# Fourteen rounds of an attention kernel issued in other orders, and six subtractions moved from GpSimd to VectorE

## The chip, the cores and the metric

The kernel runs on one core of a Trainium2 chip. Its time is the device time of one execution in microseconds, as the median of three runs. A profile is one further execution, with its own time. The core's engines each work through an instruction queue of their own, in order: TensorE (PE; its weight loads are listed as PEld), VectorE (DVE), ScalarE (ACT), GpSimd (POOL) and SyncE (SP), which here only issues transfers. An instruction waits at the head of its queue until what it needs from other engines is there, and everything behind it in that queue waits with it.

## What is computed

A gate mixes attention and a gated feed-forward block over the same input: 2048 positions, width 448, 16 heads of 28, 1792 hidden units, all float32.

```python
q, k, v = split_heads(x @ wqkv)                      # 16 heads of 28
p = softmax(einsum("bhqd,bhkd->bhqk", q, k) * 28 ** -0.5)
a = merge_heads(einsum("bhqk,bhkd->bhqd", p, v)) @ wo
gate = x @ W_gate
b = ((gate * (gate > 0)) * (x @ W_up)) @ W_down
g = sigmoid((x * gate_w).sum(-1, keepdims=True))
return g * a + (1 - g) * b
```

## The kernel before

Every operand of the projections is split into a high and a low part, and products are summed in PSUM from several terms, 11 for a projection. The program has three stages: the projections of the input (with the first maxima of scores mixed in), 32 rounds of attention, and a tail with the second half of the feed-forward block and the output.

A round `v` works on half of the 16 key blocks of head `v // 2`, for all four groups of 512 queries. One string per round (`ROUNDS`) sets the order of work, one letter a step, and it is written out by hand for rounds 0 to 10 and 29 to 31; rounds 11 to 28 take `R11` and `R12` in turn. The loop over the letters issues each step's instructions to their engines' queues in that order; no scheduler moves them afterwards. The letters are:

- `s` (`score`): two 128x512 matmuls into a pair of PSUM banks, and one read of it on ScalarE. Most scores are read by the exponential, with a bound that sits in the operands already. Those of a raw query group (`RAW`: group 3 in round 0, groups 3 and 2 in all others) are copied with their sign turned.
- `b` (`block_min`): VectorE takes the minimum of raw scores, straight from the PSUM pair for all but the first of four.
- `A` (`all_max`): seven VectorE instructions make of it one bound for every query; the last, a transpose, spreads it over the partitions (`rm`).
- `g` (`take_max`): subtracts that bound from a quad, four blocks of raw scores, 128x2048, in SBUF. GpSimd does it.
- `e`, `E` (`take_exp`): the exponential of half a quad, or of a whole one, on ScalarE.
- `P`, `Q` (`pv`): 16 products each with V, four of them side by side in the array. The profile has two records for each, 64 a round.
- `m` (`smax`): two matmuls and a VectorE maximum that prepare the bound of a later head; `n` (`smax_end`) finishes it.
- `x`: one matmul of the projections (rounds 0 to 3) or of the feed-forward block's gate and up products. After 11 of them a bank is full. ScalarE takes the gate product (`rl`), and VectorE multiplies the up product by it (`h`).
- `w`, `N`, `c`, `f`, `D`: splitting of weights, normalisation, the rescaling of a head's two halves, and the first weights of the tail.

The scores and the maxima share three pairs of PSUM banks in turn (`ps_w`), so each user of a pair waits for the readers of the user three before it. The `x` products share two single banks (`ps_x`) with the products with V. Scores run four steps ahead of their round, so a round opens with the four raw scores of its query group 2, and ends with the four of group 3 of the next round. At an odd round's start ScalarE copies the finished product with V (`ox<-po`); at an even one's VectorE adds it.

Of the kernel before, what the change touches and what calls it, by code (L numbers as in the profile page):

```python
# [8 lines left out]
F32 = mybir.dt.float32  # L9
# [3 lines left out]
OP = mybir.AluOpType  # L13
AX = mybir.AxisListType
# [4 lines left out]
P = 128  # L19
# [7 lines left out]
NF = F // P  # L27
NB = 4
# [24 lines left out]
R0 = "bsxxsbxxxxbsxxssAxxxxxxsxxsxxxmsxxgsxxxxmxsxxsxbgxxxxxxxxbEsxxemxbxxxmxeAPQ"

R1 = "nsgmsxxssNxxxxxbgxxEbbsmxxxxxxssxsxxxxAsxmxsxxxsExxxmxgmsxxxmxxxxxExmsxmgxxxxxscbssbebAPefQ"

R2 = "smsxbxxssxbxxxsgxxxsbxgxxxsmsxAxsxsxsxsmxxxxxsxmxEgxxxmmsxxbxxxsexsexgexxxxxbmexxebAxmePQ"

R3 = "nsgmsxxsgswxxbxwxxbbeAxxssxxxxxsxsxxsexmxxwxmxsNxxxsxmExmxxmxsgxxxxsxxxgmemsxxxxexsxbcbxsPebAfeQw"
# [3 lines left out]
R5 = "gsxsxxsbgsxbxxxxxwwxxxbxsmxxwxwsxssAxxxxsmxsxxxnssmxgxExmxmsxxNxxEmxxxmssgEbePbcmsbfeAxxxxxQ"

R6 = "wssbsxxxxgbsxbxxgxxxxxwxssxxxmwxsmxxsAxsxxxsxxsmxexsxeemxxxgxmsgxxemxxxmxeesseePsbwxbmQbxAx"

R7 = "ssxNxbwxgssxxxbbxxxxxAxwxswxsxxxsxxxssxmxxxxwEgxmmxnxsxsxxmsxEmxxgxmsxemxxxmgsxbsexbsecbfeAPQ"

R8 = "wxsmsbxgxxsxxswxxgxbxsbexxxsxxxssxxxAxgssxxxmxxsxmsxxxmexsxxmemegxwsxbEPmsxxbxemxsexbxAwxQ"

R9 = "sxwsNxxggswsxxxxxxxxxbsxbbxsxxsxsAxxsxxsxgemmxgxsxsxxxmxemxsxmxnEwxxwxxxmsmbEPemscxxsebfbxxAQ"

R10 = "wsxxxgssxxgxsbxxxxbxwxxxsbxwxsxxsxxsxsAsgxsxxxxmxxxemsxmxexxxmsxExxmxsmbgxxsPEebemmsbAwQ"

R29 = "sxxsxsxxxbxgxsxxbsxExsxxxxxxxxxbxssxsxAxxxsxgNxxsxsxxxssxxxxgxsxxxExxxbxgxxbxExsexxcxexfxPbAQn"

R30 = "sgsxxsbxxsxxxxxbxxgxEbxxxxxsxxxxxsssxxxxxsxxsxAsxxxxexgxxxxsxsExxxsexxxbgxxxxsexbxxsexDDbxPQA"

R31 = "sxsxxsxxxbxxxxxsbbxxxxxxxgsxxxxsxxssxxxxAsxxsxxgxgxgExxxDxxxxNxxxExxEsexcexxsxxfxxxDxPQ"
# [20 lines left out]
def gated_mix_kernel(ctx, tc, x, wq, wo, wgu, wd, out):  # L100
    nc = tc.nc
# [141 lines left out]
    AT, QUAD, slots = {}, {}, iter(range(10 ** 6))  # L243
# [43 lines left out]
    def move(dst, src):  # L287

        nc.vector.tensor_reduce(dst, src.unsqueeze(len(src.shape)), axis=AX.X, op=OP.min)

    def all_max():
        v, j, quads = todo_all.pop(0)
        to = ((0, 11) if j == 2 else (9, 10))[v % 2]
        a, b = (1 - v % 2, 9) if j == 2 else (1, 9 + v % 2)
        nc.vector.tensor_reduce(MN[:, 1:3], R2.pop((v, j)).rearrange("p a (b r) -> p a b r", r=32), axis=AX.X, op=OP.min,  # L295
                                apply_transpose=True)
        move(MN[:64, 3:5], MN[64:, 1:3])
        move(MN[:32, 5:9], MN[32:64, 1:5])
# [4 lines left out]
        nc.vector.transpose(RM[v, j], MN[:, to].unsqueeze(2).to_broadcast([P, 16, 32]))  # L303
        todo_sub.extend((v, j, q) for q in quads)

    def take_max():
        v, j, q = todo_sub.pop(0)
        m = RM[v, j].unsqueeze(1).to_broadcast([P, 4, TB])
        nc.gpsimd.tensor_tensor(QUAD[q], QUAD[q], m, op=OP.subtract)  # L309
# [55 lines left out]
    with tc.tile_pool(name="qkv", bufs=1) as pa:  # L365
# [170 lines left out]
        m, first, ahead = 0, 6, MAXIMA  # L536
# [59 lines left out]
    done = (starts[-1] - QP) // (2 * NT)  # L596
# [67 lines left out]
    RS = {}  # L664

    def rescale(v, part):

        h = v // 2
        if v % 2 == 0:
            return  # L670
        rows = slice(64, P)
        if part == 0:
            RS[h] = fe.tile([P, TB], F32, name=f"rs_{h}", tag="rb", bufs=1)
            for r, a, b in ((slice(64, 96), 11, 0), (slice(96, P), 10, 9)):
                nc.gpsimd.tensor_tensor(MN[r, 1], MN[r, a], MN[r, b], op=OP.subtract)
            nc.vector.transpose(RS[h][rows], MN[rows, 1].unsqueeze(2).to_broadcast([64, 16, 32]))
# [98 lines left out]
    for v, order in enumerate(ROUNDS):  # L775
        small_things(2 * v)
        if v == 2 * H - 3:
            early_d()
        ns = 0
        for o in order:  # L780
            if o == "s":
                ns += 1
                if ns == 6:
                    small_things(2 * v + 1)
                if ns in (1, 9) and v % 2 == 0:
                    loads(v // 2, load_k if ns == 1 else load_q)
# [153 lines left out]
    def down(i):  # L940
# [6 lines left out]
        if f == NF - 1:  # L947
# [75 lines left out]
```

## Time and profile before

| what | value |
|---|---|
| median of three runs | 1185.54 us (1185.16 to 1185.97) |
| the profiled execution | 1184.21 us, of which 1182.4 us from the first to the last instruction |
| granted TensorE clock | 0.999 of full speed |
| ScalarE, exponentials of raw scores (L320), all of them | 257.7 us |
| GpSimd, subtractions of the bound (L309) | 126 of 4.635 us |
| rounds 1 to 31 | 121.1 to 985.8 us of the span |
| the tail | 985.8 to 1182.4 us |

In the lines of the profile, an instruction is named by its line in the code, its engine and what it writes and reads: `s` scores, `sm` maxima, `qk` and `gu` the `x` products, `po` the products with V, `r` the running minimum, `rm` the spread bound, `P` and `V` the quads (two of the ten quad slots lie in a part of `V`). A row of the timeline gives start, length, engine, line, operation, and then, in brackets, how long the engine had been idle and what ended that. A row of the windows gives a stretch, its length, and each engine's busy time with the number of its instructions. A row of groups ends with busy time, mean length in ns, and idle time ahead of the group.

### The profile page before, as it was taken

What the parts mean: (1) busy time and instruction counts of PE and PEld (TensorE: products, weight loads), DVE (VectorE), ACT (ScalarE), POOL (GpSimd) and SP (SyncE); (2) the same over time, 40 slices, a digit from 0 to 9 for tenths busy, and PEclk for the clock granted to TensorE, in tenths of its full rate; (3) what the DMA queues carried; (4) which work ended last, traced back from release to release, by engine and by line L of the source; (5) the groups of instructions that cost most, each with busy time, mean ns of one, the idle gap of its engine ahead of it and who ended that gap; (6) DMA issues with size and microseconds to landing.
All of it is one profiled execution on the core that took longest, in us unless ns stands there. A gap on an engine that the chain in (4) does not pass through costs nothing.

```text
span 1182.4 us, 17006 instructions
## 1 busy us (share of the span) xinstructions
PE 1175.0 (99%) x6183; PEld 821.2 (69%) x6183; DVE 894.1 (76%) x1173; ACT 877.2 (74%) x1054; POOL 743.3 (63%) x325
## 2 busy tenths in 40 slices
PE   9999999999999999999999999999999999999998
PEld 6886666666666666666666666666666667899997
DVE  6577898888988898989898888889898553444242
ACT  5237889899999988888888887888888885322121
POOL 5323667888988886777777766767676784422020
PEclk9999999999999999999999999999999999999999
DMA  9994565636373754343446535153444437644342
GB/s 322 280 394 142 186 210 172 185 124 196 117 216 108 205 167 139 119 128 92 119 136 212 140 102 153 49 152 109 139 154 156 129 100 231 209 152 118 115 134 75
DMA packets 70667, 188.85 MB, mean 160 GB/s; under 512 B 13958, under 2 KB 20558, under 8 KB 65678
## 3 DMA queue, kind: packets, MB, share of 16 engines
q1 hardware_dynamic: 65624, 167.31, 45.9%
q0 software_dynamic: 4480, 19.99, 4.5%
q8 instruction: 48, 0.79, 0.3%
q10 hardware_dynamic: 480, 0.47, 0.1%
q14 instruction: 35, 0.29, 0.1%
HBM read 126.96 MB, written 60.96 MB: 159 GB/s over the span
## 4 chain that ended last, share of the span: by engine, by line
PE 96%; DVE 1%; DMA 1%; ACT 1%; issue 0%; SPq 0%; DVEq 0%; ACTq 0%
PE gu L633 24%; PE s L330 20%; PE po L692 19%; PE acc L927 12%; PE sm L224 10%; PE v L469 3%; PE wo L886 3%; PE qk L641 3%; PE qk L454 2%; DVE r L280 1%; DMA wr<-wq 0%; DMA X<-x_d 0%; ACT P L336 0%; ACT V L336 0%; SPq L414 0%
## 5 line engine op out<-in xcount | busy, mean ns | idle before, releaser
L309 POOL TENSOR_TENSOR P<-P,rm 128x2048 f32<-128x2048 f32 x102 | 470.8, 4635 | 107.9 <-DVE rm L303 84.1
L633 PE MATMUL gu<-X,wg 128*128 128x512 f32 x1232 | 358.9, 395 | 0.1
L228 DVE TENSOR_REDUCE mx<-sm 128x1 f32<-128x1024 f32 x256 | 302.9, 1217 | 43.0 <-PE sm L224 42.1
L330 PE MATMUL s<-Q,K 128*128 128x512 f32 x1024 | 315.9, 403 | 1.7 <-DVE mx L228 0.9
L633 PEld LDWEIGHTS gu<-X,wg 128*128 128x128 f32 x1232 | 231.2, 188 | 57.6 <-issue 1.7
L330 PEld LDWEIGHTS s<-Q,K 128*128 128x128 f32 x1024 | 180.7, 188 | 82.4 <-DVE r L280 10.4
L336 ACT ACTIVATE P<-s 128x1024 f32<-128x1024 f32 x204 | 202.2, 1028 | 42.0 <-PE s L330 39.6
L692 PE MATMUL po<-P,V 128*32 128x512 f32 x1640 | 227.4, 594 | 0.0
L334 ACT ACTIVATE P<-s 128x1024 f32<-128x1024 f32 x206 | 201.4, 1040 | 14.1 <-PE s L330 13.1
L320 ACT ACTIVATE P<-P 128x1024 f32<-128x1024 f32 (+1 forms) x182 | 208.5, 1171 | 0.5 <-POOL P L309 0.2
L224 PE MATMUL sm<-K,Q 128*128 128x512 f32 x520 | 163.2, 400 | 0.1
L280 DVE SCALAR_TENSOR_TENSOR r<-s,r 128x1024 f32<-128x1024 f32 x124 | 151.6, 1223 | 13.6 <-ACT P L336 6.0
L692 PEld LDWEIGHTS po<-P,V 128*32 128x32 f32 x1640 | 62.6, 110 | 113.3 <-issue 109.6
L692 PE MATMUL po<-V 128*32 128x512 f32 x408 | 136.2, 594 | 0.0
L309 POOL TENSOR_TENSOR V<-V,rm 128x2048 f32<-128x2048 f32 x24 | 111.2, 4635 | 26.1 <-DVE rm L303 22.6
L224 PEld LDWEIGHTS sm<-K,Q 128*128 128x128 f32 x520 | 91.9, 188 | 34.1 <-ACT P L334 4.6
L136 ACT ACTIVATE hh<-hr 128x512 fp32r<-128x512 f32 x52 | 32.8, 632 | 109.5 <-PE acc L927 109.4
L142 DVE TENSOR_TENSOR hh<-hr,hh 128x512 fp32r<-128x512 f32 x52 | 47.3, 915 | 72.6 <-ACT hh L136 72.5
L927 PE MATMUL acc<-WD,hh 128*128 128x448 f32 x480 | 99.5, 366 | 0.0
L927 PEld LDWEIGHTS acc<-WD,hh 128*128 128x128 f32 x480 | 90.2, 188 | 7.3 <-DVE hh L142 0.2
L280 DVE SCALAR_TENSOR_TENSOR r<-s,P 128x1024 f32<-128x1024 f32 x50 | 61.1, 1223 | 33.3 <-ACT P L336 33.0
L295 DVE TRANSPOSE_TENSOR_REDUCE mn<-r 128x32 f32<-128x1024 f32 x63 | 78.1, 1239 | 1.3
(93 smaller groups left out, 1135.5 us busy)
## 6 DMA issues: line engine op xcount, KB each, us to landing
wg<-ws_d SPq DMA_DIRECT2D x42, 896.0 KB
K<-qk_d SPq DMA_DIRECT2D x32, 448.0 KB
X<-x_d SPq DMA_DIRECT2D x56, 256.0 KB
h_d<-h SPq DMA_DIRECT2D x56, 256.0 KB
Q<-qk_d SPq DMA_DIRECT2D x62, 224.0 KB
hr<-h_d SPq DMA_DIRECT2D x52, 256.0 KB
ws_d<-wg SPq DMA_DIRECT2D x14, 896.0 KB
x_d<-X POOLq DMA_DIRECT2D x8, 1024.0 KB, 15.2
```

The lines of the kernel that those rows point to most:

```text
L224: nc.tensor.matmul(ps[:, c, :], Q[h][:, u * P:(u + 1) * P], K[h % 3][:, k0:k0 + TB], start=True, stop=True)
L228: nc.vector.tensor_reduce(to, ps, axis=AX.XY, op=OP.max)
L280: nc.vector.scalar_tensor_tensor(r, ps, -1.0, before, op0=OP.mult, op1=OP.min)
L295: nc.vector.tensor_reduce(MN[:, 1:3], R2.pop((v, j)).rearrange("p a (b r) -> p a b r", r=32), axis=AX.X, op=OP.min, apply_transpose=True)
L309: nc.gpsimd.tensor_tensor(QUAD[q], QUAD[q], m, op=OP.subtract)
L320: nc.scalar.activation(q, q, AF.Exp, scale=-SCALE)
L330: nc.tensor.matmul(ps[:, c], K[h % 3][:, k * P:(k + 1) * P], Q[h][:, j * TB:(j + 1) * TB], start=True, stop=True)
L334: nc.scalar.activation(dst, ps, AF.Exp, scale=SCALE)
L336: nc.scalar.activation(dst, ps, AF.Copy, scale=-1.0)
L633: nc.tensor.matmul(ps, WS[i][:, s, a], xf(i // NF, b), start=(n == 0), stop=(n == NT - 1))
L692: nc.tensor.matmul(po[32 * j:32 * j + 32], V[:, h // 4 % 2, k, h % 4], AT.pop((v, k, j)), start=(k == k0), stop=(k == k0 + NK // 2 - 1))
L927: nc.tensor.matmul(ACC[i // NF][t][:, :D], HH[i][:, a, t * P:(t + 1) * P], wd_high_low(f, b), start=(f == 0 and n == 0), stop=(f == NF - 1 ...
```

## The change

Fourteen strings are replaced (rounds 0 to 10 and 29 to 31). Each round keeps its number of `s`, `m`, `x`, `b`, `A`; some exponentials are issued as halves in place of wholes or the reverse. A new letter `G` is a `g` whose subtraction VectorE does: once in rounds 4 and 29, twice in rounds 30 and 31, six in all. Code that allows a third raw query group is added, which no entry of `RAW` uses, and a guard at the end that changes nothing here, since 52 of the 56 hidden units are finished in the rounds as before.

```diff
-RAW = [(3,), (3, 2), (3, 2), (3, 2)]
+RAW = [(3,)] + [(3, 2)] * 31
...
-R4 = "smsxxxssbxxxxswxgbwxxbxsxxgsxsAxxsswxxmxgsxexmsxxxsxxmxexsmgxxsxbxxxxxxExxbsExembxemwPQAm"
+R4 = "smsxxxsxsbxxxxxxxgsxxbbwswxxxsxsAsxwxgmxxmxxxxExsxsxsGxsExxmgxxmxxxxmsxbxxsxsbbPEAeemmwQ"
...
     def all_max():
         v, j, quads = todo_all.pop(0)
-        to = ((0, 11) if j == 2 else (9, 10))[v % 2]
-        a, b = (1 - v % 2, 9) if j == 2 else (1, 9 + v % 2)
+        c = 12 if j == 1 else 0
+        to = ((12, 21), (0, 11), (9, 10))[j - 1][v % 2]
+        a, b = (c + 1 - v % 2, c + 9) if j < 3 else (1, 9 + v % 2)
...
-    def take_max():
+    def take_max(engine):
         v, j, q = todo_sub.pop(0)
         m = RM[v, j].unsqueeze(1).to_broadcast([P, 4, TB])
-        nc.gpsimd.tensor_tensor(QUAD[q], QUAD[q], m, op=OP.subtract)
+        engine.tensor_tensor(QUAD[q], QUAD[q], m, op=OP.subtract)
         todo_exp.append(q)
...
-            elif o == "g":
-                take_max()
+            elif o in "gG":
+                take_max(nc.gpsimd if o == "g" else nc.vector)
...
-            (split_wd, 4), (fetch_w, 8), (split_wd, 5), (fetch_w, 9), (fetch_h, 7), (gate_up, done + 1)]
+            (split_wd, 4), (fetch_w, 8), (split_wd, 5), (fetch_w, 9), (fetch_h, 7)]
+    if done + 1 < NB * NF:
+        todo.append((gate_up, done + 1))
```

Three places of the order follow, on TensorE and on VectorE. The first is TensorE at the opening of round 1, behind round 0's products: `s_8_2` to `s_14_2` are its four raw scores, `sm` a maximum, `mt` the small transpose of step `n`, `qk` the `x` products. Before:

```order
L236 MATMUL mt_1112<-ident,m_711 8x128
L330 MATMUL s_8_2_1120<-Q_107,K_104 128x512 x2
L224 MATMUL sm_1127<-K_106,Q_810 128x512 x2
L330 MATMUL s_10_2_1131<-Q_107,K_104 128x512 x2
L641 MATMUL qk_1135<-X_119,wb_113 128x512 x2
L330 MATMUL s_12_2_1139<-Q_107,K_104 128x512 x2
L330 MATMUL s_14_2_1143<-Q_107,K_104 128x512 x2
```

And now:

```order
L331 MATMUL s_8_2_1113<-Q_107,K_104 128x512 x2
L224 MATMUL sm_1119<-K_106,Q_810 128x512 x2
L236 MATMUL mt_1123<-ident,m_711 8x128
L331 MATMUL s_10_2_1130<-Q_107,K_104 128x512 x2
L331 MATMUL s_12_2_1135<-Q_107,K_104 128x512 x2
L331 MATMUL s_14_2_1143<-Q_107,K_104 128x512 x2
```

The two `qk` matmuls that stood between the second and the third score now come behind the fourth, and `mt` has moved behind the first maximum; `s_12_2` takes the banks of `s_8_2`.

The second is VectorE at the opening of round 30, behind round 29's last bound: `ox` is the sum of a head's products, `mh` the end of step `n`, `r_30_2` the minima of the round's raw scores, `h` a hidden unit's product, `rq` the reciprocal of row sums. Before:

```order
L303 STREAM_TRANSPOSE rm_3_8478<-mn 128x512
L700 TENSOR_TENSOR ox<-po_8454,ox 128x512
L142 TENSOR_TENSOR mh_8501<-mt_8499,mh_8501 8x128
L280 SCALAR_TENSOR_TENSOR r_30_2_8524<-s_2_2_8512,P_2_0_8506 128x1024
L280 SCALAR_TENSOR_TENSOR r_30_2_8524<-s_4_2_8520,r_30_2_8524 128x1024
L280 SCALAR_TENSOR_TENSOR r_30_2_8524<-s_6_2_8528,r_30_2_8524 128x1024
L652 TENSOR_TENSOR h_8564<-gu_1_8543,rl_8540 128x512
```

And now:

```order
L304 STREAM_TRANSPOSE rm_3_8476<-mn 128x512
L702 TENSOR_TENSOR ox<-po_8452,ox 128x512
L142 TENSOR_TENSOR mh_8499<-mt_8497,mh_8499 8x128
L310 TENSOR_TENSOR P_3_0_8395<-P_3_0_8395,rm_3_8476 128x2048
L280 SCALAR_TENSOR_TENSOR r_30_2_8539<-s_2_2_8510,P_2_0_8505 128x1024
L280 SCALAR_TENSOR_TENSOR r_30_2_8539<-s_4_2_8515,r_30_2_8539 128x1024
L280 SCALAR_TENSOR_TENSOR r_30_2_8539<-s_6_2_8525,r_30_2_8539 128x1024
```

A subtraction from a raw quad, `P_3_0`, has come in ahead of the three minima; the other quad of the same bound, `P_3_1`, stays on GpSimd.

The third is VectorE in round 4, from the round's first bound on: `mx` are the maxima of step `m`. Before:

```order
L303 STREAM_TRANSPOSE rm_2_2020<-mn 128x512
L228 TENSOR_REDUCE mx_1658<-sm_2040 128x1
L228 TENSOR_REDUCE mx_1658<-sm_2054 128x1
L652 TENSOR_TENSOR h_2063<-gu_1_2000,rl_1986 128x512
L228 TENSOR_REDUCE mx_1658<-sm_2077 128x1
L228 TENSOR_REDUCE mx_1658<-sm_2088 128x1
```

And now:

```order
L304 STREAM_TRANSPOSE rm_2_2022<-mn 128x512
L228 TENSOR_REDUCE mx_1654<-sm_2037 128x1
L228 TENSOR_REDUCE mx_1654<-sm_2043 128x1
L653 TENSOR_TENSOR h_2048<-gu_1_1986,rl_1979 128x512
L310 TENSOR_TENSOR P_2_0_1944<-P_2_0_1944,rm_2_2022 128x2048
L228 TENSOR_REDUCE mx_1654<-sm_2083 128x1
L228 TENSOR_REDUCE mx_1654<-sm_2092 128x1
L228 TENSOR_REDUCE mx_1654<-sm_2101 128x1
```

Here too a subtraction stands ahead of the round's later maxima; the second quad of this bound stays on GpSimd, behind two of the bound before it.

More of the change, by code (lines that the diff above doesn't have):

```diff
@@ L51 @@
 R12 = "gsmsxxxxssebxxbbxxxsxxxxmxAexxssxgsxxsxxsxxmxxsxxemsmexgxexmxxxmsxmxexsbxsgebsebAPQ"
[L53 to L59, printed above, removed]
-R4 = "smsxxxssbxxxxswxgbwxxbxsxxgsxsAxxsswxxmxgsxexmsxxxsxxmxexsmgxxsxbxxxxxxExxbsExembxemwPQAm"
@@ L63 @@
[L63 to L79, printed above, removed]
+R0 = "xsbxxsxsbbxsxxxsxAxxxxsxxxsxxgsmgxxxxxxsxmxsbxxxxxxxsxxbexmxxxexsxxxbxEAmPQ"
+R1 = "smnssbbgsxxxxbAexxsxxxsxxxxgsxxsxxxsxmxsxmxNxgsxexmxsEmgxxxmxxxmxsxxmExxcxssxxxxbsebxfbxeAPQ"
@@ new lines @@
+R2 = "smsxxxsxxbxxbsgxsxxsbAxxxxxssxsgxsxxxmxxsxxmsxxEmxxxmxsxmxxsxbxxsbxxxgxxmEsgEexbAxexmPQ"
+R3 = "NsmnsxbgxssxxxebgbxxsAwxxsxxxxwsxsswgxxxxxsxmxxsxxmesexxmxxxxxcsxmgxsxbxsbsbeAxexxfxxxxeexxPmmemQw"
+R4 = "smsxxxsxsbxxxxxxxgsxxbbwswxxxsxsAsxwxgmxxmxxxxExsxsxsGxsExxmgxxmxxxxmsxbxxsxsbbPEAeemmwQ"
+R5 = "sxNxsxsgsbxxbxxxbxwxxxxxsmxxmxEsxmxxsxwxsAxxswgxxssmxxxxxxEmsxxmnxgxsmmExxxscsbxbxsgbAPefeQw"
+R6 = "sxxxsxxxssxxbbgxwbxxxsxxxemxxxmAsgxsxxxsxsxxxsmxxxesxmsxexxgmxsmexxxgxmexssePbeexbxmswQwbAw"
@@ new lines @@
+R7 = "sswxNssxxbbxbxgxxxxwxxxsxxsxEmmxswxmxxxssxxxssAxxmxgxxxmesmxexnsmgsbxxxxExcxssgfxbxbexxewAmPQ"
+R8 = "gwxsmsxxxbsxgbxxsxxxbexsAxxgsxxxxsxxssxxsxxmxxsgxxexmxxsmeewxxxwEmmxmPesmxsxxsxbxbexxsbAwQ"
+R9 = "NwgsxsxbxsxxsbxxxxxxwsbxxgswxAgxssxsxxsxxmxsxxsxmnsxxmmmxxxcmgxxExxEswxxbxxsPbmEesmxxxbeAxfQ"
+R10 = "wssxsxbgxwxbxxxsxxxxbxsxxwxxsxxsgxAxssxxxxssxxxxmxsEgmxxmxsxxmxmgxxxExsxsbsEPebebmmmwAQ"
+R29 = "NsxxssxsGxxxxxxxbEbxgxxbxsExxxxsxxxxxxsxxxxxAsxxxsxsgxxsxxxsxsxexxxxcssxxgexxbbxsxexxxxexfPbAQn"
@@ L81 @@
+R30 = "GsssxxxxxsxexxexxxbbbxxxxxAxxxxxsxsxsxxxsxxxgsxxxgxsxsGxsxxxxsxxxsEEexsxxxesbxbDbxxxxDxxxxPQA"
+R31 = "sgxxsbxxxxxsgDxxxbxsxxxxbxsxxsAxxxxxxNsExsxexxGxxsxxsxxxxxxxxxxxGexxxxxcxexxeesexsfxxxDPQ"
 ROUNDS = [
@@ L202, in raw @@
     def raw(v):
-        return RAW[v] if v < len(RAW) else RAW[len(RAW) - 2 + v % 2]
+        return RAW[v]
     def rows_of(h):
@@ L292, in all_max @@
         v, j, quads = todo_all.pop(0)
-        to = ((0, 11) if j == 2 else (9, 10))[v % 2]
-        a, b = (1 - v % 2, 9) if j == 2 else (1, 9 + v % 2)
-        nc.vector.tensor_reduce(MN[:, 1:3], R2.pop((v, j)).rearrange("p a (b r) -> p a b r", r=32), axis=AX.X, op=OP.min,
+        c = 12 if j == 1 else 0
+        to = ((12, 21), (0, 11), (9, 10))[j - 1][v % 2]
+        a, b = (c + 1 - v % 2, c + 9) if j < 3 else (1, 9 + v % 2)
+        nc.vector.tensor_reduce(MN[:, c + 1:c + 3], R2.pop((v, j)).rearrange("p a (b r) -> p a b r", r=32), axis=AX.X, op=OP.min,
                                 apply_transpose=True)
-        move(MN[:64, 3:5], MN[64:, 1:3])
-        move(MN[:32, 5:9], MN[32:64, 1:5])
+        move(MN[:64, c + 3:c + 5], MN[64:, c + 1:c + 3])
+        move(MN[:32, c + 5:c + 9], MN[32:64, c + 1:c + 5])
         nc.vector.tensor_reduce(MN[:32, to], MN[:32, a:b].rearrange("p a b -> p b a"), axis=AX.X, op=OP.min)
@@ L588, in gated_mix_kernel @@
     att = stk.enter_context(tc.tile_pool(name="att", bufs=1))
-    MN = att.tile([P, 12, 16], F32, name="mn")
+    MN = att.tile([P, 22, 16], F32, name="mn")
     nc.vector.memset(MN[:, 0], 0.0)
@@ L670, in rescale @@
             return
-        rows = slice(64, P)
+        more = 1 in raw(v)
+        rows = slice(0 if more else 64, P)
         if part == 0:
             RS[h] = fe.tile([P, TB], F32, name=f"rs_{h}", tag="rb", bufs=1)
-            for r, a, b in ((slice(64, 96), 11, 0), (slice(96, P), 10, 9)):
+            for r, a, b in ((slice(0, 32), 21, 21), (slice(32, 64), 21, 12), (slice(64, 96), 11, 0), (slice(96, P), 10, 9))[0 if more else 2:]:
                 nc.gpsimd.tensor_tensor(MN[r, 1], MN[r, a], MN[r, b], op=OP.subtract)
-            nc.vector.transpose(RS[h][rows], MN[rows, 1].unsqueeze(2).to_broadcast([64, 16, 32]))
+            nc.vector.transpose(RS[h][rows], MN[rows, 1].unsqueeze(2).to_broadcast([P - rows.start, 16, 32]))
         else:
```

## The prediction

> **What bounds the kernel now.** I read the page first, for the engine that sets the end, then four stretches as windows and the chain of work that ended last, for how long TensorE stood, and last the timelines of three round openings.
>
> ```profile
> PE 1175.0 (99%) x6183; PEld 821.2 (69%) x6183; DVE 894.1 (76%) x1173; ACT 877.2 (74%) x1054; POOL 743.3 (63%) x325
> ...
> PE 96%; DVE 1%; DMA 1%; ACT 1%; issue 0%; SPq 0%; DVEq 0%; ACTq 0%
> ```
>
> TensorE is busy for 99% and holds 96% of the chain. The change adds and removes none of its matmuls, so it moves the time by TensorE's waits alone. These are larger than the missing 1%, because a matmul's end is modelled and covers a short wait. So I count matmuls against time. The pace, from the chain:
>
> ```profile
> 510.66 7.00 PE po L692 x64
> ...
> 972.07 3.74 PE gu L633 x16
> ```
>
> I use 7.0 us for the 64 records of a round's products with V, and 0.233 us for each 128x512 matmul (3.74 / 16 is 0.234). The windows are cut where a round's last product ends: rounds 1 to 10, round 14 alone, rounds 11 to 28, rounds 29 to 31; first the length, then each engine's busy time.
>
> ```profile
> 121.08:406.88 285.80, 285.61 (x1544) 184.81 (x1543) 248.89 (x324) 261.72 (x305) 234.07 (x100) 1.00 0.54 168
> 490.69:517.66 26.97, 26.97 (x151) 17.54 (x150) 23.78 (x31) 23.39 (x26) 19.03 (x5) 1.00 0.59 167
> 406.88:905.12 498.24, 498.10 (x2719) 317.28 (x2719) 442.01 (x586) 435.05 (x491) 359.64 (x109) 1.00 0.45 136
> 905.12:985.83 80.71, 80.68 (x449) 53.11 (x447) 41.90 (x65) 71.62 (x76) 64.31 (x23) 1.00 0.38 114
> ```
>
> Rounds 1 to 10 have 898 matmuls by their strings (418 x; two for each of 160 s and 80 m): 209.2 + 70.0 = 279.2, so **6.6 us of waits, 0.66 a round**. Round 14 has 85: 19.8 + 7.0, so 0.17, the best on show. Rounds 11 to 28, which keep their order, have 1557: 362.8 + 126.0, so 9.4, 0.52 a round. Rounds 29 to 31 have 253: 58.9 + 21.0, so 0.8. At round 14's pace 4.9 us of the first stretch and 0.3 of the last could go. Round 0 has two more places:
>
> ```profile
> 94.80 0.75 issue
> ...
> 103.30 0.93 ACT P L334
> 104.23 0.04 issue
> 104.27 0.73 PE s L330 x2
> ```
>
> The chain leaves TensorE for 0.75 us ahead of the round's first score; the score at 104.27 waits for a copy on ScalarE, for at most as long. So **the orders can win at most 4.9 + 0.3 + 1.5 = 6.7 us**.
>
> **What sets a round's opening.** It has four raw scores. Three pairs of PSUM banks go round, so the third user after a score waits for that score's readers. Round 1, on TensorE, then on VectorE:
>
> ```profile
> 120.99 0.71 PE L330 MATMUL s<-Q,K 128*128 128x512 f32 x2
> ...
> 122.93 1.05 PE L330 MATMUL s<-Q,K 128*128 128x512 f32 x3
> ```
> ```profile
> 123.77 1.23 DVE L280 SCALAR_TENSOR_TENSOR r<-s,P 128x1024 f32<-128x1024 f32 x1 [0.34 <-ACT P L336]
> 125.10 2.55 DVE L280 SCALAR_TENSOR_TENSOR r<-s,r 128x1024 f32<-128x1024 f32 x2
> ```
>
> The first score's banks came free, after ScalarE's copy, for the matmul at 122.93, 1.94 us in: the time of 8 matmuls. The other three come free as VectorE's minima end, at 125.00, some 126.35 and 127.65: 4.0 to 6.7 us in, the time of about 18, 23 and 29 matmuls. These times are set by ScalarE and VectorE. **An order that has issued fewer matmuls by then waits for the difference**, 0.233 us each. I take the same four marks for every round (even ones open behind an addition on VectorE in place of a copy on ScalarE) and count the matmuls ahead of the four users, rounds 1 to 10:
>
> - before: 8/19/21/29, 9/17/22/28, 8/19/21/28, 9/17/23/27, 11/23/25/30, 10/21/23/28, 11/23/26/31, 10/20/25/30, 9/20/24/28, 12/22/26/30. The largest shortfalls are 2, 1, 2, 2, 0, 1, 0, 0, 1, 0: in all 9.
> - after: 6/16/21/27, 9/18/22/29, 8/17/21/27, 9/21/25/30, 9/22/24/28, 12/20/25/30, 7/20/24/27, 10/21/25/31, 11/19/23/27, 13/20/26/30. They are 2, 1, 2, 0, 1, 0, 2, 0, 2, 0: in all 10.
>
> **Part by part**, against the profiled execution's 1184.21 us, 1.33 under the median of 1185.54; the sum is added to either alike.
>
> 1. Openings of rounds 1 to 10: one matmul more, +0.23 us. Rounds 4 and 6 win; 5, 7 and 9 lose. Round 29 had 14/18/22/34 and has 9/22/28/36: -0.23.
> 2. Round 0. ScalarE's order up to the copy at 103.30 is the same in both, and so is what holds it. Ahead of the matmul that waits for it the old order has 35 of the round's matmuls, the new one 33: +0.47. One is put ahead of the first score, into the wait of 0.75; that buys nothing, since the later wait ends no sooner.
> 3. Six subtractions move from GpSimd to VectorE: one each in rounds 4 and 29, two each in 30 and 31.
>
> ```profile
> L309 POOL TENSOR_TENSOR P<-P,rm 128x2048 f32<-128x2048 f32 x102 | 470.8, 4635 | 107.9 <-DVE rm L303 84.1 <-DVE rq L707 12.9 <-ACT P L320 4.9
> ...
> L142 DVE TENSOR_TENSOR hh<-hk,hh 128x512 fp32r<-128x512 f32 x4 | 2.7, 674 | 2.4 <-ACT hh L136 2.4
> ...
> L278 DVE TENSOR_TENSOR r<-P,r 128x1024 f32<-128x1024 f32 x2 | 2.5, 1226 | 0.2
> ```
>
> VectorE takes 0.674 us for 512 columns and 1.226 for 1024, so about 1.226 + 2 x 0.552 = 2.3 for 2048, against 4.6 on GpSimd. But both operands lie in SBUF, and such an instruction does not run beside one of GpSimd. In the tail:
>
> ```profile
> 1127.47 2.42 POOL L145 TENSOR_TENSOR on<-or,on 128x1024 fp32r<-128x1024 f32 x1 [32.74 <-ACT on L136]
> 1127.94 2.50 DVE L142 TENSOR_TENSOR hh<-hr,hh 128x512 fp32r<-128x512 f32 x1 [3.17 <-ACT hh L136]
> ```
>
> VectorE's subtraction took 2.50 us in place of 0.674: it ended at 1130.44, 0.55 after GpSimd's. VectorE's present work in rounds 1 to 31 has an operand in PSUM or no second one, so the rounds don't show this yet. A moved subtraction costs VectorE between 2.3 and 2.3 + 4.6 = 6.9 us, and what stands behind it comes late. Round 30, GpSimd and then VectorE:
>
> ```profile
> 932.43 9.21 POOL L309 TENSOR_TENSOR P<-P,rm 128x2048 f32<-128x2048 f32 x2 [0.76 <-DVE rm L303]
> ```
> ```profile
> 931.57 0.71 DVE L303 STREAM_TRANSPOSE rm<-mn 128x512 f32<-128x512 f32 x1
> 932.98 0.69 DVE L700 TENSOR_TENSOR ox<-po,ox 128x512 f32<-128x512 f32 x1 [0.70 <-PE po L692]
> 933.59 0.27 DVE L142 TENSOR_TENSOR mh<-mt,mh 8x128 fp32r<-8x128 f32 x1
> 935.58 1.23 DVE L280 SCALAR_TENSOR_TENSOR r<-s,P 128x1024 f32<-128x1024 f32 x1 [1.72 <-ACT P L336]
> ```
>
> GpSimd starts on the first of two subtractions as soon as `rm` is there, 932.43. The change gives the other to VectorE behind `mh`, at 933.86, and ahead of the round's minima. It would stand until 937.1 and end near 939.3 (2.2 after, as in the tail). The minima then end at 940.5, 941.8 and 943.0 and not from 936.8 on: 7.7, 9.0 and 10.2 us into the round, the time of 33, 39 and 44 matmuls, where the new order has 29, 32 and 35. Shortfall 9 matmuls, 2.1 us. An `rm` that comes earlier shortens it, to nothing if by more than 2 us; I take +1.9.
>
> Round 4 stands as follows. GpSimd has two subtractions ahead, until 221.3 where its present rows have them; VectorE comes to its own after `rm`, two maxima and a product, near 221.4.
>
> ```profile
> 212.04 13.82 POOL L309 TENSOR_TENSOR P<-P,rm 128x2048 f32<-128x2048 f32 x3
> ```
>
> Behind it stand three maxima, whose first pair of banks is wanted 17.5 us into the round. If VectorE is first, nothing waits; if GpSimd has just begun its third, the maxima come 6.9 us later and TensorE waits 3.6. I take +1.2, a meeting a third of the way, as the two come so close. Round 29's comes right behind `rm`, ahead of GpSimd; round 31's two come when GpSimd has finished: nothing, and at most 2.9 (below).
>
> The Trainium skill ("SBUF — State Buffer", section "SBUF: two separate sides") says that GpSimd and VectorE hold a pair of ports exclusively, and that the later one blocks for the whole instruction. The rows at 1127 agree; by a free sharing of the ports this term would be about nothing.
>
> 4. The other waits of rounds 1 to 10, 6.6 - 9 x 0.233 = 4.5 us, lie at restarts and among later maxima. The new order may remove 2.8 of it (4.9 less the openings' 2.1) or add as much. The nearest row is the unchanged rounds', 0.52 against 0.66; reaching it gives -1.4. I take half, -0.7.
>
> The products wait for no subtraction now, and in the new order the nearest subtraction stands 6.7 us of TensorE's time ahead of its product (6.4 before): nothing. Were that cover gone, GpSimd's 4.6 us would show at a product. The tail is the same.
>
> Sum: 0.23 - 0.23 + 0.47 + 1.9 + 1.2 - 0.7 = **+2.9 us**: 1187.1 for the profiled execution, 1188.4 for the median.
>
> **The rivals.**
> - *The two engines do not collide* (0.32): `rm` comes two us earlier, or the ports let both through. Terms 1, 2 and 4 are left, -0.2: 1185.3, no change. For it: 6.9 us is the worst meeting, and the new orders shift both engines. Against it: in round 30 GpSimd needs nothing but `rm`, and VectorE has two instructions in between.
> - *The waits do go* (0.18): faster. Copies and minima come free for the new users in all rounds as in round 14 now, and nothing collides: half of the 6.7 us goes, 1182.2. It decides where the marks 8/18/23/29 move with the order. Against it: 10 matmuls of shortfall where there were 9.
> - *A hidden unit's product stands behind a subtraction too*: its bank is wanted again after 11 matmuls of the other and some six of scores, 4.0 us, so a full 6.9 costs 2.9 more: 1191.3. It is the upper part of the forecast's own case.
> - *The change does not do what it says*: at the openings the distance is not larger. That is in the forecast already.
>
> **How the numbers follow.** A measurement of this kernel tells about 0.2%, 2.4 us, from no change. The forecast (0.50) reaches from 1186.5 to 1191.3 and lies for the most part, not all, beyond 1187.9: slower 0.40. Within: its lower part and the first rival, 0.42. Faster: 0.18. The range runs from the middle of the faster case to just under the product's: 1182.4 to 1190.8.
>
> **What would show it.** Subtractions on VectorE that take 2.3 us where GpSimd rests, and 4 to 7 where it works, the first of round 30 above all; behind it TensorE waits near 940 to 943. No waits at the opening of round 4 and some near its end. The windows: rounds 1 to 10 within 284 to 288 us, 29 to 31 over 82. Wrong would be subtractions of 2.3 us beside a busy GpSimd, or banks that are free after 6 or 16 matmuls in round 1.

## The result, and the profile after

The changed kernel takes 1194.26 us (median, 1192.97 to 1194.62) against 1185.76 us before: a ratio of the means of 1.0068, 95% interval 1.0055 to 1.0081. The forecast was 1188.4 (1182.4 to 1190.8): the sign was right, the size too small by 5.9 us, and the time lies 3.5 us above the range. The profiled execution of the changed kernel took 1192.97 us with a span of 1191.2, 8.76 us over the one before.

Engines and chain on the page of the changed kernel:

```profile
PE 1178.0 (99%) x6183; PEld 820.8 (69%) x6183; DVE 921.3 (77%) x1179; ACT 877.5 (74%) x1054; POOL 721.5 (61%) x319
...
PE 90%; DVE 3%; DMA 2%; ACT 2%; issue 1%; POOL 0%; SPq 0%; ACTq 0%; DVEq 0%; POOLq 0%
```

TensorE has the same 6183 records, and holds 90% of the chain where it held 96%. These 6% are not the size of its waits: at a wait the chain goes over to the work of the engine that ended it. Two of the moved subtractions now lie on the chain, nearly whole (start, length, engine, tile, line):

```profile
223.01 6.22 DVE P L310
...
940.31 5.63 DVE P L310
```

The waits are read from the windows, cut as before where a round's last product ends (length first): rounds 1 to 10, 11 to 28, 29 to 31.

```profile
121.71:413.53 291.82, 288.16 (x1547) 185.17 (x1544) 255.62 (x325) 261.56 (x302) 229.14 (x100) 0.99 0.52 163
413.53:911.50 497.97, 497.88 (x2722) 317.23 (x2719) 441.66 (x585) 435.12 (x491) 360.44 (x110) 1.00 0.45 137
911.50:994.60 83.10, 81.44 (x451) 52.84 (x447) 60.87 (x70) 71.97 (x79) 46.98 (x18) 1.00 0.33 111
```

Rounds 1 to 10 take 6.0 us more than before (285.80), rounds 29 to 31 2.4 more (80.71); the unchanged rounds 0.3 less (498.24), and round 0 ends 0.6 later (121.08). The sum is 8.8. By single rounds, as waits, that is a round's length between starts on TensorE less 0.231 us for each of its matmuls and 7.0 for its products (so worked out from the records, us; the prediction's 0.233 a matmul would make every sum lower, rounds 1 to 10 before at 6.6 in place of 8.1). The column of round 0 holds everything up to that round's end less a constant, so its differences alone count:

| kernel | 0 | 3 | 4 | 7 | 9 | 29 | 30 | 31 | all others |
|---|---|---|---|---|---|---|---|---|---|
| before | 10.30 | 0.78 | 0.75 | 0.90 | 0.96 | 0.61 | 0.29 | 0.29 | 16.8 |
| changed | 11.04 | 2.05 | 4.97 | 1.56 | 1.29 | 0.60 | 2.70 | 0.28 | 16.1 |

Two rounds lose most, 4 and 30, and both have a subtraction on VectorE; round 3, which has none, is third. First VectorE of the changed kernel (start, length, engine, line, operation), then GpSimd:

```profile
222.93 6.30 DVE L310 TENSOR_TENSOR P<-P,rm 128x2048 f32<-128x2048 f32 x1
229.16 3.47 DVE L228 TENSOR_REDUCE mx<-sm 128x1 f32<-128x1024 f32 x3
...
912.52 2.29 DVE L310 TENSOR_TENSOR P<-P,rm 128x2048 f32<-128x2048 f32 x1
...
940.24 5.70 DVE L310 TENSOR_TENSOR P<-P,rm 128x2048 f32<-128x2048 f32 x1
945.86 1.21 DVE L280 SCALAR_TENSOR_TENSOR r<-s,P 128x1024 f32<-128x1024 f32 x1
...
953.66 6.27 DVE L310 TENSOR_TENSOR P<-P,rm 128x2048 f32<-128x2048 f32 x1
```
```profile
222.42 4.65 POOL L310 TENSOR_TENSOR V<-V,rm 128x2048 f32<-128x2048 f32 x1
...
912.94 6.39 POOL L310 TENSOR_TENSOR P<-P,rm 128x2048 f32<-128x2048 f32 x1 [6.80 <-DVE rm L304]
...
939.16 4.64 POOL L310 TENSOR_TENSOR P<-P,rm 128x2048 f32<-128x2048 f32 x1 [1.01 <-DVE rm L304]
```

Where VectorE comes second, its subtraction ends 2.1 us after GpSimd's (229.23 against 227.07; 945.94 against 943.80), so it stood until GpSimd was through and then took its own time. In round 29 VectorE is first, at 912.52: it takes 2.29, and GpSimd's, begun 0.42 later, is the one that stands (6.39 in place of 4.6). Round 30's second subtraction, at 953.66, stands behind GpSimd too (6.27), and TensorE shows no wait behind it until 969 us: nothing behind it in VectorE's queue was needed in that time. What the others do on TensorE:

```profile
181.77 0.73 PE L331 MATMUL s<-Q,K 128*128 128x512 f32 x2 [0.60 <-ACT V L337]
...
230.42 0.73 PE L331 MATMUL s<-Q,K 128*128 128x512 f32 x2 [2.61 <-DVE mx L228]
231.00 1.18 PE L634 MATMUL gu<-X,wg 128*128 128x512 f32 x3
231.97 1.05 PE L331 MATMUL s<-Q,K 128*128 128x512 f32 x2
232.83 0.63 PE L634 MATMUL gu<-X,wg 128*128 128x512 f32 x1
...
947.13 0.73 PE L331 MATMUL s<-Q,K 128*128 128x512 f32 x2 [0.88 <-DVE r L280]
948.46 0.72 PE L331 MATMUL s<-Q,K 128*128 128x512 f32 x2 [0.37 <-DVE r L280]
949.79 0.74 PE L331 MATMUL s<-Q,K 128*128 128x512 f32 x2 [0.37 <-DVE r L280]
```

In round 30 the three minima come late, one score after the other. In round 4 a score waits for the first late maximum: 3.0 us lie between two starts (227.42 and 230.42), 2.8 more than the pace; and behind it the matmuls stand 0.43 us apart (231.97 to 232.83 is two of them), not 0.23. The granted clock says why (windows of 2 us; the third number from the right):

```profile
228.00:230.00 2.00, 0.00 (x0) 0.00 (x0) 2.00 (x2) 0.67 (x1) 0.00 (x0) 1.00 0.24 80
230.00:232.00 2.00, 1.58 (x6) 1.24 (x7) 2.00 (x3) 2.00 (x3) 0.00 (x0) 0.84 0.78 213
232.00:234.00 2.00, 2.00 (x6) 1.30 (x4) 1.85 (x2) 1.57 (x2) 0.00 (x0) 0.50 0.96 234
234.00:236.00 2.00, 2.00 (x17) 0.56 (x20) 1.77 (x2) 1.74 (x3) 0.00 (x0) 0.81 0.57 152
```

So round 4's 4.2 us are 2.8 of waiting and some 1.3 of half clock (five matmuls with 0.2 more each, and 0.33 ahead of the products). This is one profile; whether the clock falls there in the other executions too, no record shows. The row at 181.77 is a third loss: round 3's second raw score waits for ScalarE's copy of the first.

### The profile page after: what moved, and what is told of

Same layout as the page of the kernel before. It is cut to its first block, busy times and chain, and to the rows that moved or that the text cites. A ratio compares the mean times of both kernels' runs of the same rounds, so it can differ in the third digit from the quotient of the medians.

```text
span 1191.2 us, 17005 instructions
## 1 busy us (share of the span) xinstructions
PE 1178.0 (99%) x6183; PEld 820.8 (69%) x6183; DVE 921.3 (77%) x1179; ACT 877.5 (74%) x1054; POOL 721.5 (61%) x319
## 4 chain that ended last, share of the span: by engine, by line
PE 90%; DVE 3%; DMA 2%; ACT 2%; issue 1%; POOL 0%; SPq 0%; ACTq 0%; DVEq 0%; POOLq 0%
PE gu L634 22%; PE s L331 19%; PE po L694 19%; PE acc L929 11%; PE sm L224 10%; PE wo L888 3%; PE qk L642 3%; PE v L470 2%; DVE r L280 1%; DVE P L310 1%; DMA Q<-qk_d 1%; ACT P L337 1%; DMA wr<-wq 0%; DMA ox<-x 0%; ACT P L335 0%
## 5 line engine op out<-in xcount | busy, mean ns | idle before, releaser
L310 POOL TENSOR_TENSOR P<-P,rm 128x2048 f32<-128x2048 f32 x96 | 445.0, 4650 | 116.5 <-DVE rm L304 90.6
```

The costliest lines, as they stand in the source:

```text
L310: engine.tensor_tensor(QUAD[q], QUAD[q], m, op=OP.subtract)
```

## The experiments

The theory going in: VectorE's subtraction stands behind GpSimd's (A). Its rivals: the new orders themselves cost the time (B); VectorE's longer queue, or what GpSimd is relieved of, decides (C). The waits by rounds of all runs are in a table at the end of this section.

**All subtractions back on GpSimd.** In rounds 4, 29, 30 and 31 each `G` becomes `g`:

```diff
-R30 = "GsssxxxxxsxexxexxxbbbxxxxxAxxxxxsxsxsxxxsxxxgsxxxgxsxsGxsxxxx...
+R30 = "gsssxxxxxsxexxexxxbbbxxxxxAxxxxxsxsxsxxxsxxxgsxxxgxsxsgxsxxxx...
```

> The changed kernel with all six subtractions back on GpSimd, the new orders kept. Theory A (VectorE's subtractions stand behind GpSimd's): round 4's waits fall from 4.97 to about 0.8 us and round 30's from 2.70 to about 0.3, the other rounds stay, so 1194.3 - 6.6 = 1187.7 us (1187 to 1188.5). Rival B (the new orders cost the time, wherever the subtractions run): within 1 us of 1194.3. Rival C (VectorE's longer queue helps elsewhere, since GpSimd is relieved): between them, with new waits in rounds 29 to 31.

Measured: 1194.18 us, ratio 1.0076 (1.0063 to 1.0089). Rounds 4 and 30 fall to 0.85 and 0.29 as A says; but round 29 rises from 0.60 to 4.67 and round 31 from 0.28 to 2.56, and the total stays. It is the total that B named, though not by B's cause: two gains and two losses cancel. Round 29 on TensorE, ScalarE and GpSimd:

```profile
922.54 0.73 PE L331 MATMUL s<-Q,K 128*128 128x512 f32 x2 [1.85 <-ACT V L335]
923.12 0.40 PE L634 MATMUL gu<-X,wg 128*128 128x512 f32 x1
923.94 1.22 PE L331 MATMUL s<-Q,K 128*128 128x512 f32 x2 [0.43 <-ACT P L335]
```
```profile
919.67 1.91 ACT L321 ACTIVATE P<-P 128x2048 f32<-128x2048 f32 x1 [1.75 <-POOL P L310]
921.48 1.01 ACT L335 ACTIVATE V<-s 128x1024 f32<-128x1024 f32 x1
```
```profile
910.40 9.23 POOL L310 TENSOR_TENSOR P<-P,rm 128x2048 f32<-128x2048 f32 x2 [6.48 <-DVE rm L304]
```

GpSimd does two subtractions in a row, to 919.6; ScalarE's exponential waits for the second, the exponential that frees a score's banks stands behind it, and TensorE waits for those banks. So A holds in rounds 4 and 30, and C in 29 and 31: there the new order asks for a subtraction sooner than GpSimd alone gives it, and VectorE's turn at it, which costs nothing there, is worth 4.07 + 2.28, some 6.3 us in this profile. Of the 4.07 some 1.6 are a half clock that another kernel with the same order did not have (last section), so it is 4.8 to 6.3.

**Both subtractions of a bound on VectorE**, in rounds 4 and 30, the second behind the three maxima or minima, so that GpSimd has none of these two bounds (a later bound of round 30 is still shared):

```diff
-R4 = "...sxsxsGxsExxmgxxmxxxxmsxbxx...
+R4 = "...sxsxsGxsExxmxxmxxxxmsGxbxx...
-R30 = "GsssxxxxxsxexxexxxbbbxxxxxAxxxxxsxsxsxxxsxxxgsxxxgx...
+R30 = "GsssxxxxxsxexxexxxbbbGxxxxxAxxxxxsxsxsxxxsxxxsxxxgx...
```

> The changed kernel, with the other quad's subtraction of the same bound on VectorE too in rounds 4 and 30 (behind the three maxima, and behind the three minima), so that GpSimd has nothing to collide with there; VectorE has two more subtractions. Theory A: the first subtraction of either round takes 2.3 us in place of 6.30 and 5.70; round 4's waits fall to about 1 us, round 30's to about 0.5, round 5's opening may lose 0.2: 1194.3 - 6.2 = 1188.1 us (1187.3 to 1189). Rival B (orders): 1194.3. Rival C (a subtraction of 2048 columns takes VectorE about six us in these places whoever else works, or VectorE's queue is simply too long): 1194.3 or more, up to 1199.

Measured: 1188.22 us, ratio 1.0024 (1.0015 to 1.0033). VectorE has more to do, and the kernel is 6.0 us faster than the changed one by the medians, 5.2 by the ratios:

```profile
223.14 2.27 DVE L310 TENSOR_TENSOR P<-P,rm 128x2048 f32<-128x2048 f32 x1
...
936.76 2.27 DVE L310 TENSOR_TENSOR P<-P,rm 128x2048 f32<-128x2048 f32 x1
```

The same two instructions, at the same places, take 2.27 us in place of 6.30 and 5.70. Neither VectorE's queue nor the place makes them long, but GpSimd beside them. Round 4 falls to 0.59, round 30 to 0.79, although the subtraction of the bound that is still shared takes 6.30 us at 948.82; round 5 loses 0.6 where 0.2 was expected (with this string its third raw score gets the pair of the first again, after two users).

**Round 4's subtraction one maximum earlier:**

```diff
-R4 = "...AsxwxgmxxmxxxxExsxsxsGxsExxmg...
+R4 = "...AsxwxgmGxxmxxxxExsxsxsxsExxmg...
```

> The changed kernel with round 4's subtraction on VectorE one maximum earlier, so that VectorE comes to it some 1.1 us before GpSimd ends its second subtraction and can start its third. Theory A, if the engine that already waits gets the ports first: VectorE's row ends near 224.6 in place of 229.2, round 4's waits fall from 4.97 to about 1.2 us, 1190.6 us (1190 to 1191.5). Theory A, if GpSimd goes on with its third: VectorE's row takes about 8 us, round 4 loses 3 us more, 1197. Rivals B and C: 1194.3 within 0.7, since one place in the queue changes neither the order's distance nor the length.

Measured: 1191.74 us (1.0055, 1.0042 to 1.0068): 2.5 us less than the changed kernel by the medians, 1.5 by the ratios, whose intervals overlap; it is the waits that show it, 2.51 in round 4 in place of 4.97. In VectorE's queue the subtraction now also stands ahead of a hidden unit's product. VectorE, GpSimd, TensorE:

```profile
221.89 3.43 DVE L310 TENSOR_TENSOR P<-P,rm 128x2048 f32<-128x2048 f32 x1
```
```profile
213.95 9.23 POOL L310 TENSOR_TENSOR P<-P,rm 128x2048 f32<-128x2048 f32 x2
223.13 6.65 POOL L310 TENSOR_TENSOR V<-V,rm 128x2048 f32<-128x2048 f32 x1
```
```profile
226.51 0.73 PE L331 MATMUL s<-Q,K 128*128 128x512 f32 x2 [1.22 <-DVE mx L228]
```

VectorE waits for GpSimd's second to end (223.18) and is through at 225.32; GpSimd's third, next in its queue, stands for VectorE's two us and takes 6.65. So in this case the engine that already waited went next. Another score now waits, 1.4 us, and round 4 keeps 2.51 where 1.2 was expected; the time is 0.2 us above the range expected.

**Round 3's opening.** The built programs name the pair of banks of each tile. They are not handed out strictly in turn: `ps_w` takes every third pair from one pool, and the others from a pool of two. In the changed kernel round 3's second raw score has the same pair as its first, with one maximum between them; in no other of the rounds 1 to 31, before or after, is the pair of such a score given again so soon. Step `n` put first changes the pairs (on top of all subtractions on GpSimd):

```diff
-R3 = "NsmnsxbgxssxxxebgbxxsA...
+R3 = "NnsmsxbgxssxxxebgbxxsA...
```

> As orders_only, with step n of round 3 ahead of the round's first raw score, by which the second raw score gets another pair of banks than the first (in the changed kernel it takes the first one's own pair, two users on and not three). Theory: the wait of 0.85 us at round 3's second raw score goes, round 3's waits fall from 2.05 to about 1.0 us, so 1.0 us less than orders_only: 1186.7 us. Rival (ScalarE is late there and any user would wait): no change against orders_only, and the wait stays near 181.8 us or moves to the next score.

Measured: 1193.62 us (1.0072, 1.0060 to 1.0084), 0.6 under that kernel, within the intervals, where 1.0 was expected. Round 3 falls from 2.06 to 1.10, but `n`'s transpose now waits for ScalarE's copy of the products, and round 2's account rises by 0.76. So once more, the maximum first and `n` left third, with rounds 4 and 30 back on GpSimd:

```diff
-R3 = "NsmnsxbgxssxxxebgbxxsA...
+R3 = "NmsnsxbgxssxxxebgbxxsA...
```

> The changed kernel with rounds 4 and 30 back on GpSimd, and round 3 opened with the maximum ahead of the first raw score, step n still third: the second raw score then has a pair of its own and step n does not stand first, where it waited 0.72 us for ScalarE's copy of the products. Theory (round 3's wait is the pair given again after two users): waits of rounds 2 and 3 together fall from 2.77 to about 1.5 us, so 1.2 us under the same kernel without this edit (1188.8): 1187.6 us. Rival (ScalarE, still busy with the products' copy at the round's opening, is late for any order): 2.6 us in rounds 2 and 3, 1188.8.

Measured: 1187.43 us, ratio 1.0026 (1.0015 to 1.0037), where the same kernel without this edit has 1.0025 (below). Intervals of 0.0011 either way, 1.3 us, can't tell the 1.2 us of the theory from nothing; the waits can. Rounds 2 and 3 together lose 2.4 us in place of 2.8, where the theory had 1.5. The wait at the second score is gone, and another stands in its place:

```profile
184.19 0.73 PE L331 MATMUL s<-Q,K 128*128 128x512 f32 x2 [0.27 <-DVE r L280]
184.76 0.63 PE L642 MATMUL qk<-X,wb 128*128 128x512 f32 x2
185.52 0.73 PE L331 MATMUL s<-Q,K 128*128 128x512 f32 x2
```

These two scores come 0.44 and 0.30 us later than the pace, and round 3 still waits 1.72. The pair explains where round 3 waited, not that it waits: 0.3 of its 1.3 us. What the rest hangs on stays open.

**Rounds 29 and 31 on VectorE, 4 and 30 on GpSimd** (each `G` of rounds 4 and 30 becomes `g`):

> The changed kernel with round 4's and round 30's subtractions back on GpSimd and those of rounds 29 and 31 left on VectorE. Theory (the move costs in rounds 4 and 30, where GpSimd is at work, and pays in rounds 29 and 31, whose new orders ask for a subtraction before GpSimd alone can give it): round 4 near 0.85, round 30 near 0.3, rounds 29 and 31 near 0.6 and 0.3, so 1194.3 - 6.5 = 1187.8 us (1187 to 1188.6). Rival (rounds 29 to 31 share one delay that only moves about, so that putting round 30's back brings a wait of two us or more in round 29 or 31): 1190 or more.

Measured: 1188.79 us, ratio 1.0025 (1.0015 to 1.0035): rounds 4, 29, 30 and 31 at 0.80, 0.59, 0.29 and 0.28, as expected; the time is 0.2 us above the range expected, and in the profile round 0 ends 0.8 us later than in the changed kernel's. Against the kernel before, rounds 0, 3, 7 and 9 are left.

**The old strings in those rounds and in round 1:**

```diff
-R0 = "xsbxxsxsbbxsxxxsxAxxxxsxxxs...
+R0 = "bsxxsbxxxxbsxxssAxxxxxxsxxs...
-R7 = "sswwNssxxbbxbxgxxxxwxxxsxxs...
+R7 = "ssxNxbwxgssxxxbbxxxxxAxwxsw...
...
```

> As that, with the old orders put back in rounds 0, 1, 3, 7 and 9, where the changed kernel waits longer than the one before; the new orders stay in rounds 2, 4, 5, 6, 8, 10 and 29 to 31. Theory (waits belong to the round's own string and add up): round 0 near 10.3, rounds 1 to 10 near 7.7 in all (8.1 before, 14.1 in the changed kernel), rounds 29 to 31 near 1.2: 1185.2 us, within 0.2% of the kernel before. Rival (a round's waits hang on what the rounds before it did to the bank pairs and queues): one or more of the old strings waits 0.5 us longer than it did, 1186.5 to 1188.

Measured: 1189.05 us, ratio 1.0031 (1.0021 to 1.0042): the rival, and 1 us more than the rival had. Rounds 0, 1, 3 and 9 are what they were before, but round 7 keeps 1.37 with its old string (0.90 before), and rounds 4 and 8, whose strings stayed new, rise to 1.59 and 2.67. At round 3's opening `n`'s transpose waits 0.72 us for ScalarE's copy of the products, which the same string did not do before; it stands in round 2's account. Round 8 on TensorE, ScalarE, GpSimd:

```profile
342.81 0.62 PE L694 MATMUL po<-V 128*32 128x512 f32 x1 [0.52 <-ACT V L321]
```
```profile
341.70 2.01 ACT L321 ACTIVATE V<-V 128x1024 f32<-128x1024 f32 x2 [2.11 <-POOL V L310]
```
```profile
329.55 2.82 POOL L145 TENSOR_TENSOR wg<-wgr,wg 128x384 fp32r<-128x384 f32 x3
332.45 9.22 POOL L310 TENSOR_TENSOR V<-V,rm 128x2048 f32<-128x2048 f32 x2
```

GpSimd is late with its subtractions, ScalarE's exponential waits for them, and the product waits for the exponential. So the waits of a string hang on what the strings ahead of it leave to the queues.

**The late rounds alone:** strings of before in rounds 0 to 10, of the changed kernel in 29 to 31.

> The kernel before in rounds 0 to 10, the changed one in rounds 29 to 31, with their five subtractions on VectorE. Theory: round 30 alone loses, 2.4 us: 1185.7 + 2.4 = 1188.1 us (1187.5 to 1188.8). Rival (round 30's loss needs the lag that the early rounds leave): 1185.7.

Measured: 1187.90 us, ratio 1.0020 (1.0011 to 1.0029). Round 30 waits 2.67, 29 and 31 nothing new: as expected.

**The kernel before, with a matmul put ahead of each waiting user:**

```diff
-R4 = "...xxbxsxxgsxsAxxsswxxmx...
+R4 = "...xxbxsxxxgssAxxsswxxmx...
-R11 = "...Amxsxxemsxmxexxmxsmxxemmgexsb...
+R11 = "...Amxsxxemsxxmexxmxsmxxemmgexsb...
...
```

> The kernel before, with one matmul of a hidden unit moved ahead of the waiting score in rounds 1, 3, 4 and 9 (waits of 0.16 to 0.23 us and a restart of 0.1 there) and of the waiting maximum in round 11's string, which rounds 13, 17, 21 and 25 use too (0.12 and 0.11). Theory (an opening waits for the matmuls that it lacks, one at a time): each wait goes, 1.25 us in rounds 1 to 9 and 0.95 in the others: 1185.5 - 2.2 = 1183.3 us. Rival (the wait moves to the next user of the same readers): no change, 1185.5; halfway is 1184.4.

Measured: 1185.97 us against 1185.85, ratio 1.0003 (0.9994 to 1.0012): the rival. Round 1 gains 0.23 and round 3 0.09; in rounds 4, 9, 13 and 17 a later user waits 0.11 to 0.16 us in place of the one that was helped, and rounds 15, 19 and 23, which share round 11's string and had no such wait, lose 0.2 each. Round 4's score here comes 0.34 us after the matmul ahead of it, and the pace is 0.23. The profile names no releaser; ScalarE copies without a pause from 216.29 to 220.99, so it is taken to wait for one of these copies:

```profile
218.86 0.40 PE L633 MATMUL gu<-X,wg 128*128 128x512 f32 x1
219.20 0.73 PE L330 MATMUL s<-Q,K 128*128 128x512 f32 x2
```

Waits by rounds, us, of the profiled executions:

| kernel | 0 | 3 | 4 | 7 | 9 | 29 | 30 | 31 | all others |
|---|---|---|---|---|---|---|---|---|---|
| all on GpSimd | 11.50 | 2.06 | 0.85 | 1.77 | 1.28 | 4.67 | 0.29 | 2.56 | 17.2 |
| both on VectorE | 11.26 | 2.03 | 0.59 | 1.60 | 1.27 | 0.62 | 0.79 | 0.28 | 16.7 |
| one maximum earlier | 11.73 | 2.05 | 2.51 | 1.58 | 1.27 | 0.59 | 2.72 | 0.28 | 15.8 |
| all on GpSimd, `n` first | 10.83 | 1.10 | 0.80 | 1.77 | 1.28 | 3.08 | 0.29 | 2.56 | 17.9 |
| 29 and 31 on VectorE | 11.81 | 2.06 | 0.80 | 1.76 | 1.29 | 0.59 | 0.29 | 0.28 | 17.6 |
| the same, maximum first | 10.69 | 1.72 | 0.86 | 1.78 | 1.32 | 0.63 | 0.29 | 0.28 | 16.6 |
| the same, old strings | 10.42 | 0.76 | 1.59 | 1.37 | 0.97 | 0.58 | 0.29 | 0.28 | 19.3 |
| late rounds alone | 10.33 | 0.78 | 0.76 | 0.90 | 0.96 | 0.61 | 2.67 | 0.28 | 16.7 |
| before, matmuls ahead | 11.19 | 0.69 | 0.74 | 0.90 | 0.95 | 0.59 | 0.32 | 0.29 | 17.8 |

No kernel that was run is faster than the one before, and none points to one that would be.

## Why the prediction was wrong in size

Of the 5.9 us that were missing, 3.0 are round 4's, 1.2 the openings' and 1.1 those of the other waits of rounds 1 to 10; 0.5 are round 30's, and what is left are small differences.

- **What bounds** was right: the same matmuls, and 8.8 us of new waits on TensorE.
- **Term 3, round 30** (+1.9): right. The meeting is close to the worst one, VectorE 1.1 us behind GpSimd's start; it ended 2.14 after GpSimd, and TensorE lost 2.4. The round's second moved subtraction stands in no sentence of the term; it met GpSimd as well (6.27 us) and cost nothing.
- **Term 3, round 4** (+1.2) is the step that failed most. Which instructions meet was right, and so were the bounds, nothing to 3.6; "a meeting a third of the way" had no row behind it. GpSimd began its third subtraction at 222.42 and VectorE came 0.51 later: nearly the worst case. TensorE waited 2.8, and then ran at half clock for 1.3 more, a cost that stood in no term: 4.2 in all. With both subtractions on VectorE all of it is gone; theory A had that kernel's time to 0.1 us.
- **Rounds 29 and 31** (nothing): right as a difference, and wrong in what it passed over. The prediction costed the move of each subtraction against the old orders; in the new ones these moves are what keeps rounds 29 and 31 from losing 4.8 to 6.3 us. The -0.23 of round 29's opening did not come: 0.61 before, 0.60 after.
- **Term 1, openings** (+0.23): the waits at those users were 0.9 us in rounds 1 to 10 before and 2.3 after, so +1.4. Most of it is the 0.85 of round 3, where "the third user after a score waits" did not hold: the pair came round after two. But with pairs as assumed, round 3 gained only 0.3. Apart from that pair, users waited in rounds where the marks had put a shortfall (1, 3, 4 and 9 before; 1, 2, 3, 5, 7 and 9 after), 0.16 to 0.30 us each; rounds 2 and 6 before, one matmul short, lost next to nothing. And matmuls put ahead of waiting users in the old orders moved the waits to the next ones. The marks 8, 18, 23 and 29 say where a wait appears, not that time is gained when one is met.
- **Term 2, round 0** (+0.47): the waits at the three places behind 94 us are 1.12 us against 1.01, so about +0.1 (with the 0.1 us by which the matmul behind a late one comes late too, 1.2 to 1.3 in the four profiles with the old string and 1.4 to 1.6 in the seven with the new). The other half us of round 0 lies near 46 us, where the orders are the same: a wait for a transfer of Q, 0.98 in the changed kernel, 0.20 before, but 1.10 in the last run above, which has the old order. No instruction order differs ahead of it, so it is taken as no part of the change; but the seven profiles with the new round 0 have 0.7 to 1.6 us there, the four with the old 0.2 to 1.1, and why is not shown.
- **Term 4** (-0.7): rounds 1 to 10 lost 6.0 us in all, and with round 4's 4.2 and the openings' 1.4 taken off about 0.4 is left at most, so the gain did not come. Rounds 1 to 10 without 3 and 4 went from 6.6 to 7.1, their openings included: rounds 2, 5, 6, 8 and 10 did gain, 0.06 to 0.2 each, and rounds 1, 7 and 9 lost 0.13, 0.66 and 0.33. What holds round 7 was not tried alone; its waits are a dozen of some 0.1 us, half of them at maxima.
- **The rivals.** "The two engines do not collide" and "the waits do go" both fell; the third, a hidden unit's product behind a subtraction, showed nowhere in the changed kernel. The range ended at 1190.8, just under that third case. With round 4 at its own upper bound the sum would have been 1190.8 already, so the range left no room for any other term to miss.
- **The signs.** The subtraction of round 30 took 5.70 us beside GpSimd, and rounds 29 to 31 came to 83.1 us (over 82), both as forecast. Rounds 1 to 10 came to 291.8, not to 284 to 288.

## What to carry to other kernels

Two instructions that exclude each other must be taken at the worst meeting unless a row shows a margin larger than the drift of both queues: in round 4 VectorE came half a microsecond too late, and the round lost 4.2 us. Such a meeting costs only what is soon needed behind the instruction that stands; the one at 953.66 cost nothing. In rounds 4 and 30, giving all of one bound's work to one engine, whichever, was better than sharing it between two that exclude each other. A new order and a moved instruction have to be costed together: in rounds 29 and 31 the new order loses 4.8 to 6.3 us without the move and nothing with it. And where readers of a buffer set the pace, work put ahead of one waiting user can make a later one wait.

## What the runs showed of the hardware

The clock that TensorE is granted fell to half after waits of 2.3 to 2.6 us, and not after each of them. With all subtractions on GpSimd, round 29 waits 1.85 and 0.43 us; in the two kernels with that order the same pair of waits (1.84 and 0.44 in the other) was followed by different clocks. The first such kernel, from 922 us on, and the one with `n` first in round 3, from 921 on:

```profile
922.00:924.00 2.00, 1.03 (x4) 0.54 (x4) 0.39 (x1) 2.00 (x4) 2.00 (x1) 0.98 0.00 0
924.00:926.00 2.00, 2.00 (x5) 1.61 (x6) 1.01 (x2) 2.00 (x3) 1.78 (x4) 0.50 0.71 115
926.00:928.00 2.00, 2.00 (x8) 1.59 (x7) 0.00 (x0) 1.67 (x2) 2.00 (x1) 0.67 0.97 375
```
```profile
921.00:923.00 2.00, 1.10 (x4) 0.62 (x5) 0.48 (x1) 2.00 (x4) 2.00 (x1) 1.00 0.00 0
923.00:925.00 2.00, 2.00 (x9) 1.58 (x10) 0.92 (x2) 2.00 (x3) 1.78 (x4) 1.00 0.63 125
```

Round 29 costs 4.67 in the one and 3.08 in the other. Cut finer, the clock stands at 0.50 from 231.35 to 234.76 in the changed kernel's round 4 and from 923.92 to 927.33 here: 3.41 us both times, and begun 0.9 and 1.4 us after TensorE had started again. After the wait of 1.4 us in round 4 with the subtraction one maximum earlier, the clock stayed at 1.00. The Trainium skill ("TensorE: Matmul & The Clock Gate", section "What's actually happening") has the clock fall after an idle window of some 3.4 us that runs free of the program. The length of the half clock and the two outcomes of one wait agree with windows that run free; that a whole window must be idle does not: 2.3 us with three matmuls in between were enough here.

The subtraction of VectorE and that of GpSimd, both operands in SBUF, exclude each other in both directions: 6.30 us in place of 2.27 on VectorE, 6.39 in place of 4.6 on GpSimd. In the one place where both queues had work, the engine that already waited went ahead of the other's next instruction: 3.43 and 6.65 us in round 4 with VectorE one maximum earlier.
